# Mixed mLSTM attention and mixture-of-experts kernel: two raw weight tiles decoded later, another order of units 0 to 5, other places for w1's loads

## Chip, cores and metric

One core of one Trainium2 chip runs the whole program. The metric is the device time of one execution in microseconds; the median of several runs is given. The kernel issues all of its instructions by hand-written orders on five engines: PE (TensorE), DVE (VectorE), ACT (ScalarE), POOL (GpSimd) and SP (SyncE, which issues the loads).

## The reference

Three stages follow one another. The first is an mLSTM attention over 4 batches, 8 heads, 768 tokens and heads of 40, which the kernel computes in chunks of 128 tokens:

```python
for t in range(S):
    m_new = np.maximum(f_gate[:, :, t] + m, i_gate[:, :, t])
    f_stab = np.exp(f_gate[:, :, t] + m - m_new)
    i_stab = np.exp(i_gate[:, :, t] - m_new)
    C = f_stab * C + i_stab * np.einsum('bhd,bhe->bhde', vt, kt)
    n = f_stab * n + i_stab * kt
    h_tilde = np.einsum('bhde,bhe->bhd', C, qt)
    denom = np.maximum(np.abs(nq), 1.0)
    y[:, :, t] = sigmoid(o_gate[:, :, t]) * h_tilde / denom
```

The second is a soft mixture of experts over the 3072 tokens of width 320: logits against phi, a softmax over the tokens for each of 32 slots, 8 experts with w1 (320 x 1024) and w2 (1024 x 320) on the slots, and a softmax over the slots to mix back:

```python
slot_input = softmax(x @ phi, over tokens).T @ x
h = np.maximum(slot_input[e] @ w1[e], 0.0)
slot_out[e] = h @ w2[e]
x = softmax(x @ phi, over slots) @ slot_out
```

The third is a feed-forward block of width 1024 on every token:

```python
h = x @ w_in
solu = h * softmax(h)
ln = (solu - mu) / np.sqrt(var + 1e-06) * g_ln
return ln @ w_out
```

w_in and w_out come as 64-bit floats; the kernel takes their bits and builds 32-bit floats on the chip.

## The kernel before

**Attention.** There are 24 units, unit i being chunk i // 4 of batch i % 4. Each has one load of q and k (`load_qk`, three DMAs into 3 buffers) and one of k, v and the output gate (`load_kvo`, 484 KB into 4 buffers). A unit's work is a list of short names, in an order written out by hand: `FIRST` for units 0 to 5, `ORDER[i % 4]` for the others; `ops(i)` maps each name to a function. Every engine issues its own instructions in that order, so a name that stands earlier in the list goes earlier into its engine's queue. In unit i, `R` (`pe_decay`, lines 229 to 234) makes the decays of unit i + 2 with PE: for each half of the heads a product of `gl` and `gr` (L233) and one that adds the causal mask (L234). `exp` takes their exponential on ACT, `scA` and `scB` make the scores of unit i + 1 on PE (L265), `wA` and `wB` multiply the two on DVE into `lb` (L269), `o0` to `o3` are unit i's products with the values (L283) and with the state C (L286), `u0` to `u3` the update of the state (L293). `num`, `den`, `sg` and `x` form the output of unit i - 1; `numa` is a copy of PE's result on ACT (L308) in chunk 0 and sums on DVE from chunk 1 on, `C` is the new state (ACT L339 in chunk 0, DVE L341 behind that).

**Gates.** The gates of all 768 tokens of a chunk row are worked on together on 128 partitions: `gate(lo, hi, k)` (lines 166 to 191) is step k of eight, a scan for the maxima (L170), subtractions, cumulative sums (L181), and at last step 7, which adds the last sum of each chunk, and step 8, which builds the decays of whole chunks (`dec`, L191). Tokens 0 to 127 are done ahead of unit 0, 128 to 255 in unit 0 (names `GA`), and 256 to 767 in units 0 to 5 (names `GB`), 512 columns at once; for these step 7 runs on POOL (L189) and step 8 on DVE, over four chunks. `gate_hi` and `gate_lo` split a value in a high and a low part, `gate_right` (L211, POOL, for chunks 1 and 2; ACT for later ones) and `gate_left` (L216, ACT) spread them into `gr` and `gl`, `pe_gate` and `gate_nat` turn them for the chunk's use. The tiles `gt`, `m`, `gp` and `dec` of the gates lie in the pool `p1`, which is closed after the attention.

**Decoding.** Ten raw tiles of 512 KB (`load_raw`, lines 455 on), five of w_in and five of w_out, are loaded in the odd units 1 to 19 into two buffers in turn (`raw_t` and the last tile of `w1s`, which w1 needs last). Raw n is decoded in units 2n + 2 and 2n + 3 by `decode` (lines 462 to 480): `D0` are two DVE instructions (L469, L470), `D1` and `D1b` two on ACT (L472, L474), `D2` and `D3` two on DVE (L476, L478), and `D4` one product on POOL (L480).

**Loads.** All loads are issued by SP in one queue, each once its place is free. Each unit's loads of the unit after next go first, then one w1 tile of 512 KB at the end of the units in `W1_UNITS` (18 of them; the first of the 19 tiles of `w1s` is loaded ahead of unit 0's work, and a twentieth, `w1l`, goes in unit 22 into the place of `raw_t`). w2 of expert 0 is loaded after unit 21, the seven others (1280 KB each) when the attention is over, in the order 2, 4, 6, 1, 3, 5, 7, into the pool `tl`, which takes the place of the closed pools `p1` and w1s. A tile's load waits until every user of each tile that lay there is done.

**Tail.** The products with w1 (L787), then those with w2 (L831; the even experts first, eight and then 56 products, and 64 for the odd ones), then the mixing back. Between them `wo` loses its mean (L834), is copied into `wh` on ACT (L839), and the rest goes to `wl` on DVE (L840); behind that DVE copies the result of w2, `so` (L848). At last a loop over 24 tiles of 128 tokens does the feed-forward block (from L898 on); there the elementwise tiles `e` have three buffers in the pool `fin`.

## Time and profile before

| | us |
|---|---|
| median of 3 runs (lowest, highest) | 299.53 (298.48, 299.69) |
| the profiled execution | 295.74 |
| its span | 293.6 |
| busy in the span: PE, DVE, ACT, POOL | 274.5, 236.8, 214.5, 151.8 |

The profile is one execution, recorded by the hardware; the span runs from its first instruction to its last. Its granted TensorE clock is 1.00 all the way, the full of its two levels (2.4 GHz). "Busy" counts an engine's instructions, and PE's are modelled at their ends. A page of the profile gives totals, costliest groups of instructions and a chain: the work that ended last, followed back through what released it. Other views take a stretch of time or a line of the code. The loads' share is the mean busy share of the core's 16 DMA engines. The attention runs from about 10 to 144 us, the tail to 178 us, and the last loop to the end.

### The profile page before, as it was taken

The numbers are of one execution on the slowest core, as the hardware profiler recorded it, in microseconds if no ns is written. First come the engines' busy times: TensorE is split into PE (matmuls) and PEld (weight loads), VectorE is DVE, ScalarE is ACT, GpSimd is POOL, SyncE is SP. The second block draws the span as 40 slices with busy tenths as digits, with TensorE's granted clock in tenths as the row PEclk, the third lists the DMA queues.
The fourth block names the chain that finished last, engine by engine and source line by source line (L and its number), as shares of the span: only waits on it lengthen the run. The fifth ranks groups of instructions, "written<-read, shape, count | busy, mean of one in ns | idle before, by whom it ended". The sixth has DMA issues, their size and how long they took to land.

```text
span 293.6 us, 8341 instructions
## 1 busy us (share of the span) xinstructions
PE 274.5 (93%) x3245; PEld 219.5 (75%) x3245; DVE 236.8 (81%) x499; ACT 214.5 (73%) x482; POOL 151.8 (52%) x180
## 2 busy tenths in 40 slices
...
GB/s 160 251 298 265 285 284 198 211 341 291 291 257 292 284 307 246 278 298 362 369 364 361 169 2 0 0 119 111 104 90 99 104 89 100 103 88 99 106 82 47
DMA packets 48791, 57.28 MB, mean 195 GB/s; under 512 B 26800, under 2 KB 38704, under 8 KB 48752
## 3 DMA queue, kind: packets, MB, share of 16 engines
...
q14 instruction: 13, 0.11, 0.1%
HBM read 47.03 MB, written 3.93 MB: 174 GB/s over the span
## 4 chain that ended last, share of the span: by engine, by line
PE 74%; DMA 10%; DVE 9%; ACT 2%; POOL 2%; SPq 1%; issue 1%; POOLq 0%; ACTq 0%
PE o L982 10%; PE o L979 10%; PE o L980 9%; PE po L283 6%; PE sc L265 6%; DMA qk<-qkp 4%; PE uT L944 3%; PE pr L286 3%; PE h L898 3%; PE so_ph L831 3%; DMA gt<-gates 3%; DMA w1s<-w1p 3%; PE xTp L350 2%; PE R L233 2%; PE R L234 2%; PE dps L293 2%
## 5 line engine op out<-in xcount | busy, mean ns | idle before, releaser
L979 PE MATMUL o<-wh,uh 128*128 128x320 f32 x192 | 60.0, 318 | 0.0
L980 PE MATMUL o<-wl,uh 128*128 128x320 f32 x192 | 57.9, 307 | 0.0
L982 PE MATMUL o<-wh,ul 128*128 128x320 f32 x192 | 47.6, 308 | 0.0
L950 POOL COPY up<-u 128x1024 uint16<-128x1024 uint16 x22 | 23.3, 1060 | 45.1 <-issue 23.0
L283 PE MATMUL po<-kvo,lb 128*64 128x41 f32 x768 | 38.3, 229 | 5.1 <-ACT num L308 3.4
L283 PEld LDWEIGHTS po<-kvo,lb 128*64 128x64 f32 x768 | 30.6, 137 | 11.5 <-ACT num L308 3.8
L980 PEld LDWEIGHTS o<-wl,uh 128*128 128x128 f32 x192 | 36.1, 188 | 1.0
L979 PEld LDWEIGHTS o<-wh,uh 128*128 128x128 f32 x192 | 36.0, 188 | 0.9
L960 POOL COPY uf<-tp 128x1024 uint16<-128x1024 uint16 x22 | 35.3, 1605 | 2.5 <-DMA tp<-up 2.4
L917 DVE SCALAR_TENSOR_TENSOR u<-h,e 128x1024 f32<-128x1024 f32 (+1 forms) x25 | 29.4, 1181 | 9.0 <-ACT e L910 8.9
L265 PE MATMUL sc<-qk 64*128 64x128 f32 x384 | 31.5, 288 | 2.3 <-DMA qk<-qkp 1.2
L982 PEld LDWEIGHTS o<-wh,ul 128*128 128x128 f32 x192 | 33.0, 187 | 0.1
L269 DVE TENSOR_TENSOR lb<-sc,lb 128x512 f32<-128x512 f32 x48 | 31.3, 675 | 1.7 <-PE sc L265 1.7
L265 PEld LDWEIGHTS sc<-qk 64*128 64x128 f32 x384 | 25.3, 187 | 8.9 <-issue 4.3
L903 DVE TENSOR_REDUCE st<-h 128x1 f32<-128x1024 f32 x24 | 29.3, 1220 | 1.4 <-PE h L898 1.4
L246 ACT ACTIVATE kvo<-kvo 128x320 f32<-128x320 f32 x48 | 22.6, 471 | 8.6 <-DMA kvo<-kvo 6.0
L910 ACT ACTIVATE e<-h,st 128x1024 f32<-128x1024 f32 (+1 forms) x25 | 26.7, 1069 | 2.8 <-DVE st L903 2.6
L929 ACT ACTIVATE e<-u,st 128x1024 f32<-128x1024 f32 x24 | 27.4, 1141 | 0.0
L238 ACT ACTIVATE lb<-R 128x1024 f32<-128x1024 f32 x24 | 24.4, 1015 | 3.6 <-PE R L234 3.5
L986 ACT ACTIVATE ob<-o,st 128x320 f32<-128x320 f32 x24 | 12.7, 528 | 18.8 <-ACT e L910 13.6
L254 POOL TENSOR_TENSOR kvo<-kvo,nat 128x320 f32<-128x320 f32 x24 | 19.8, 825 | 10.6 <-PE sc L265 4.5
L233 PE MATMUL R<-gr,gl 128*128 128x512 f32 x48 | 22.8, 531 | 1.1 <-ACT lb L238 0.7
...
## 6 DMA issues: line engine op xcount, KB each, us to landing
...
```

What stands on the lines that cost most here:

```text
L233: PE.matmul(U[u]["R"][:, a], gl_t[c % 2][:, b, :], gr_t[c % 2][:, a * NR:(a + 1) * NR, :], start=True, stop=False)
L265: PE.matmul(U[u]["sc", a][:, r, :], t[p, 0, r, :], t[p, 1, r, :], start=True, stop=True)
L269: V.tensor_tensor(out=lb[:, a * NR:(a + 1) * NR, :], in0=U[u]["sc", a], in1=lb[:, a * NR:(a + 1) * NR, :], op=ALU.mult)
L283: PE.matmul(U[u]["po"][t, 2 * r + a, :], U[u]["lb"][:, a * NR + r, t], va(u, 2 * r + a), start=True, stop=True)
L903: V.tensor_reduce(out=F[i]["st"][:, 0:1], in_=F[i]["h"], axis=AX.XY, op=ALU.max, negate=True)
L910: A.activation(out=F[i]["e"][:, c], in_=F[i]["h"].rearrange("p n f -> p (n f)")[:, c], func=AF.Exp, bias=st[:, 0:1], accum_out=st[:, acc:a ...
L917: V.scalar_tensor_tensor(out=F[i]["u"][:, c], in0=F[i]["h"].rearrange("p n f -> p (n f)")[:, c], scalar=1.0, in1=F[i]["e"][:, c], op0=ALU. ...
L929: A.activation(out=F[i]["e"], in_=F[i]["u"], func=AF.Square, bias=st[:, 3:4], accum_out=st[:, 5:6])
L960: G.tensor_copy(out=uf.rearrange("p k t -> p (k t)").bitcast(U16).rearrange("p (n two) -> p n two", two=2), in_=F[i]["tp"].rearrange("p tw ...
L979: PE.matmul(o, uh, wh[:, k, :], start=k == 0, stop=False)
L980: PE.matmul(o, uh, wl[:, k, :], start=False, stop=False)
L982: PE.matmul(o, ul, wh[:, k, :], start=False, stop=k == FC - 1)
```

## The change

Nothing is computed differently. What changes is places and orders:

- The tiles of the gates (`gt`, `m`, `gp`, `dec`) move from the pool `p1` into a permanent tile `ga` of 2560 columns. After the gates are done its first 2048 columns take raw tiles 3 and 4, and in the last loop two of the three buffers of `e`. `p1` becomes shorter, and the places of `w1s` and of the w2 tiles against each other shift.
- In the attention only eight raw tiles are decoded (`RAWS`: 5, 6, 7, 8, 9, 0, 1, 2, in units 6 to 21; the two buffers change roles). Raws 3 and 4 are loaded at the ends of units 16 and 18 (`LATE`) and decoded by `late_decode`, which stands behind w2's products and ahead of `wh` and `wl`.
- `FIRST` is written anew: no decodes in units 2 to 5; the copies of num and C of chunk 0's units stand at the end of their own unit; steps of the gates stand later, step 5 in two parts; all of `left` for chunk 2 in unit 5.
- The load of the gates of tokens 256 to 767 stands behind that of q and k of unit 3, no longer ahead of it.
- `gate_right` for chunks 1 and 2 is one DVE instruction of 64x1024 in place of two on POOL of 64x512. The lower half of `gr`'s second tile is copied on POOL and not on ACT.
- Steps 7 and 8 of the gates run for one chunk at a time, on DVE, when `ops(i)` is called for units 6, 8, 12 and 16.
- `pe_decay` issues both products with `gl` and then both with the causal mask.
- `W1_UNITS`: no w1 load ahead of unit 1, two at the ends of units 4 and 5, one in each of the units 6 to 15, then units 17 and 22; `w1l` in unit 20.

```diff
--- before
+++ after
...
  "D1b xT numa R C numb scA D3 D1 scB o0 den0 sig0 cd den1 u3 D2 den2 wA D4 o3 u0 sig1 sg exp wB xTc u1 u2 o1 o2 lraw x sig2 kw right",
 )
 FIRST = (
- "q4 o0 u0 o1 u1 L0 R o2 u2 o3 u3 exp L1 wA wB kw sig0 sig1 sig2 left GA7 GA8 GB1",
- "scA numa scB C den0 den2 sg x o0 u0 o1 u1 wA R o2 u2 wB exp o3 u3 sig0 right0 kw right1 GB2 GB3 lraw k4 sig1 sig2",
- "q5 xT numa scA C scB den0 xTc den2 sig0 R o0 sg x o1 gn gnc u3 wA o3 kw wB GB4 o2 exp u1 u2 u0 sig1 D0 GB5 sig2 ph",
- "k5 q6 D1b xT numa C scA D1 scB o0 den0 den2 sg x sig0 D2 D3 u3 wA GB6 R D4 o3 u0 sig1 exp wB xTc u1 GH0 u2 o1 o2 lraw sig2 kw",
- "k6 R sig0 numa GH1 GL0 scA C xT scB den0 den2 o0 u0 xTc exp wB o3 o2 GL1 sg wA right0 cd o1 sig1 x D0 right1 u1 u2 u3 kw sig2 lfa gl",
- "q7 k7 D1b xT C numa numb R scA D1 D3 den0 xTc den2 sig0 lfb D2 scB kw sg wA o0 wB x u1 cd o3 lt o2 sig1 u3 o1 u2 D4 exp lraw ltc u0 tm0 GB7 GB8 sig2",
+ "q4 o0 u0 o1 u1 L0 R o2 u2 o3 u3 exp n0 c0 L1 wA wB kw GA7 GA8 right0 sig0 sig1 sig2 left",
+ "scA scB den0 den2 sg x o0 u0 o1 u1 wA R o2 u2 wB exp o3 u3 n1 c1 kw k4 GB1 sig0 sig1 sig2 ph GB2",
+ "q5 xT scA scB den0 xTc den2 o0 sg x o1 R gn gnc u3 wA o3 kw wB o2 exp u1 u2 u0 n2 c2 GB3 GB4 sig0 sig1 GB5a sig2",
+ "k5 q6 xT scA scB den0 xTc den2 o0 sg x o1 R u3 wA o3 kw wB o2 exp u1 u2 u0 n3 c3 GB5b GB6 sig0 GH0 sig1 sig2",
+ "k6 R sig0 GH1 scA xT scB den0 den2 o0 u0 xTc sg x exp wB o3 o2 wA cd o1 GL0 GL1 right0 sig1 u1 u2 u3 kw sig2 gl",
+ "q7 k7 xT C numa numb R scA den0 xTc den2 sig0 left scB kw sg wA o0 wB x u1 cd o3 lt o2 sig1 u3 o1 u2 exp lraw ltc u0 tm0 sig2",
 )
-W1_UNITS = (0, 2, 3, 4, 6, 7, 8, 9, 10, 12, 13, 14, 15, 16, 18, 19, 20, 21)
+W1_UNITS = (1, 2, 3, 4, 4, 5, 5, 6, 7, 8, 9, 10, 11, 12, 13, 14, 15, 17, 22)
+RAWS = (5, 6, 7, 8, 9, 0, 1, 2)
+RAW1 = 6
+LATE = {16: 3, 18: 4}
 HALVED = (0,)
 FIN_START = "h:0 m:0 w:2 e0:0 e1:0 h:1 m:1 u0:0 u1:0 w:2 T0:0 e:1 T1:0 u:1 x0:0 y0:0 x1:0 h:2 m:2 y1:0 v:0 v:1 e:2"
 FIN = "o:-1 u:2 d:2 t:2 h:3 m:3 q:0 k0:0 T0:1 T1:1 k1:0 x0:1 g:1 x1:1 y1:0 y0:1 k2:0 k3:0 s:0 a4:0 a5:0 e:3 a6:0 a7:0 v:1 b4:0 b5:0 b6:0 b7:0"
 DT = range(2, 24)
+HALF = (slice(0, 64), slice(64, 128))
 ENG = {"x": "G", "cd": "G", "kw": "G", "sg": "V", "D4": "G", "C": "V", "xTc": "A"}
 
 
...
     nat = cpool.tile([128, NU, NS], F32, tag="nat", name="nat")
     gl_t = [cpool.tile([128, NB, T], F32R, tag=f"gl{n}", name=f"gl{n}") for n in range(2)]
     gr_t = [cpool.tile([128, NH, T], F32R, tag=f"gr{n}", name=f"gr{n}") for n in range(2)]
+
+    ga = cpool.tile([128, 2560], F32, tag="ga", name="ga")
 
     w1_ctx = ExitStack()
     w1pool = w1_ctx.enter_context(tc.tile_pool(name="w1pool", bufs=1))
...
     cd_t = fixed("cd", [128, NR, 2 * DV])
     C_t = [fixed("Cl", [128, NR, 2 * DV])] + C_t
     dsc_t = fixed("dsc", [128, 512], 1, I32)
-    gt_t = fixed("gt", [128, 2, S])
-    m_t = fixed("m", [128, S + 1], 1, F32R)
-    dec_t = fixed("dec", [32, NC, 16])
-    gp_t = fixed("gp", [128, T], 1, F32R)
-    fixed("gap", [128, 112])
+    gt_t = ga[:, 0:2 * S].rearrange("p (k t) -> p k t", k=2)
+    m_t = ga[:, 2 * S:3 * S + 1].bitcast(F32R)
+    gp_t = ga[:, 2308:2308 + T].bitcast(F32R)
+    dec_t = ga[0:32, 2440:2440 + 16 * NC].rearrange("p (c j) -> p c j", c=NC)
+    fixed("gap", [128, 96])
     dps = ps_o.tile([128, NR, 2 * DV], F32, tag="dps", name="dps")
 
     def load_qk(u):
...
             last = gf[0:32].rearrange("p (c t) -> p c t", t=T)[:, :, T - 1:T]
             if k == 7:
                 g = gi[0:32].rearrange("p (c t) -> p c t", t=T)
-                (G if lo > T else V).tensor_tensor(out=g, in0=g, in1=last.to_broadcast([32, n, T]), op=ALU.add)
+                V.tensor_tensor(out=g, in0=g, in1=last.to_broadcast([32, n, T]), op=ALU.add)
             else:
                 V.tensor_tensor(out=dec_t[:, lo // T:hi // T], in0=m16.unsqueeze(1).to_broadcast([32, n, 16]), in1=last.to_broadcast([32, n, 16]), op=ALU.mult)
 
...
             for j in js:
                 A.activation(out=gr_t[c % 2][0:64, j, :], in_=x[0:64], func=AF.Copy, scale=hsel[0:64, j:j + 1])
             return
-        G.tensor_tensor(out=gr_t[c % 2][0:64, js], in0=x[0:64].unsqueeze(1).to_broadcast([64, NR, T]), in1=hsel[0:64, js].unsqueeze(2).to_broadcast([64, NR, T]), op=ALU.mult)
+        V.tensor_tensor(out=gr_t[c % 2][0:64], in0=x[0:64].unsqueeze(1).to_broadcast([64, NH, T]), in1=hsel[0:64].unsqueeze(2).to_broadcast([64, NH, T]), op=ALU.mult)
 
     def gate_left(c, js=range(NB)):
         p = slice(64, 128)
...
         U[u]["R"] = ps_sc.tile([128, 2, NR, T], F32, tag="R", name=f"R{u}")
         for a in range(2):
             PE.matmul(U[u]["R"][:, a], gl_t[c % 2][:, b, :], gr_t[c % 2][:, a * NR:(a + 1) * NR, :], start=True, stop=False)
+        for a in range(2):
             PE.matmul(U[u]["R"][:, a], eyeb, causal.to_broadcast([128, NR, T]), start=False, stop=True)
 
     def st_exp(u):
...
     def load_w1(n):
         SP.dma_start(out=w1s[:, n, :], in_=w1p[n])
 
-    raws = (w1s[:, 18, :].bitcast(I32).rearrange("p (n two) -> p n two", two=2), raw_t)
-
-    def load_raw(n):
-        raw = raws[n % 2]
+    raws = (raw_t, w1s[:, 18, :].bitcast(I32).rearrange("p (n two) -> p n two", two=2))
+
+    def load_raw(n, raw):
         SP.dma_start(out=raw, in_=w64[n].bitcast(I32).rearrange("p (n two) -> p n two", two=2))
         RAW[n] = raw
 
...
     def decode(n, k):
         lo, hi = RAW[n][:, :, 0].bitcast(U32), RAW[n][:, :, 1]
         f = win[:, n, :] if n < 5 else wo.rearrange("p f d -> p (f d)")[:, 512 * (n - 5):512 * (n - 4)]
-        if k == 0:
+        if (n, 0) not in RAW:
             RAW[n, 0] = dsc_t
         sc = RAW[n, 0]
         if k == 0:
...
     load_kvo(1)
     load_qk(2)
     load_kvo(2)
-    load_gates(2 * T, S)
     G.tensor_copy(out=gl_t[0][0:64], in_=bsel[0:64].unsqueeze(2).to_broadcast([64, NB, T]))
     A.copy(out=gr_t[0][64:128], in_=hsel[64:128].unsqueeze(2).to_broadcast([64, NH, T]))
     G.tensor_copy(out=eyeb, in_=ident)
...
     for a in range(2):
         pe_scores(0, a)
     load_qk(3)
+    load_gates(2 * T, S)
     load_kvo(3)
-    load_w1(0)
     pe_decay(0)
     st_exp(0)
     pe_gate(0)
...
     st_exp(1)
     for a in range(2):
         pe_scores(1, a)
-    A.copy(out=gr_t[1][64:128], in_=hsel[64:128].unsqueeze(2).to_broadcast([64, NH, T]))
     for a in range(2):
         st_w(0, a)
     st_sig(0)
...
         G.memset(x[:, DM + 1:384], 0.0)
         G.memset(x[:, DM:DM + 1], 1.0)
     G.tensor_copy(out=gl_t[1][0:64], in_=bsel[0:64].unsqueeze(2).to_broadcast([64, NB, T]))
+    G.tensor_copy(out=gr_t[1][64:128], in_=hsel[64:128].unsqueeze(2).to_broadcast([64, NH, T]))
     G.memset(sbd, 0.0)
 
     def load_phi():
...
         if nx2:
             T["R"] = lambda: pe_decay(i + 2)
             T["exp"] = lambda: st_exp(i + 2)
-        dn = (i - 2) // 2 if 1 <= i < 22 else -1
-        if dn >= 0:
+        dn = (i - RAW1) // 2
+        if 0 <= dn < len(RAWS):
             if i % 2 == 0:
-                T["D0"] = lambda: decode(dn, 0)
+                T["D0"] = lambda: decode(RAWS[dn], 0)
             else:
                 for n, k in (("D1", 1), ("D1b", 1.5), ("D2", 2), ("D3", 3), ("D4", 4)):
-                    T[n] = lambda k=k: decode(dn, k)
+                    T[n] = lambda k=k: decode(RAWS[dn], k)
         if i < 6:
             for k in range(1, 9):
                 T[f"GA{k}"] = lambda k=k: gate(TOK, 2 * TOK, k)
...
                 T[f"L{k}"] = lambda k=k: gate_lo(TOK, 2 * TOK, k)
                 T[f"GH{k}"] = lambda k=k: gate_hi(2 * TOK, S, k)
                 T[f"GL{k}"] = lambda k=k: gate_lo(2 * TOK, S, k)
-                T[f"right{k}"] = lambda k=k: gate_right(i // 4 + 1, slice(NR * k, NR * k + NR))
+            T["right0"] = lambda: gate_right(i // 4 + 1, None)
+            T["GB5a"], T["GB5b"] = lambda: gate(2 * TOK, 4 * TOK, 5), lambda: gate(4 * TOK, S, 5)
+            T[f"n{i}"], T[f"c{i}"] = lambda: st_num(i, (0,)), lambda: st_state(i)
         elif b and c + 2 < NC:
             js = range(4 * b - 8, 4 * b - 4) if c == 1 else range(3 * b - 3, min(3 * b, NH))
             T["right"] = lambda: gate_right(c + 2, js)
-        T["lfa"], T["lfb"] = lambda: gate_left(2, (0, 1)), lambda: gate_left(2, (2, 3))
-        nl = {0: 1}.get(i, c + 1 if b == 0 and i > 4 else NC)
+        nl = {0: 1, 5: 2}.get(i, c + 1 if b == 0 and i > 4 else NC)
         if nl < NC:
             T["left"] = lambda: gate_left(nl)
         ng = {2: 1, 6: 2}.get(i, c + 1 if b == 0 and i > 4 else NC)
         if ng < NC:
+            if ng > 1:
+                for k in range(7, 9):
+                    gate(ng * TOK, ng * TOK + TOK, k)
             T["gn"] = lambda: pe_gate(ng)
             T["gnc"] = lambda: gate_nat(ng)
-        if i % 2 == 1 and i < 20:
-            T["lraw"] = lambda: load_raw((i - 1) // 2)
+        if i % 2 == 1 and 0 <= i + 1 - RAW1 < 2 * len(RAWS):
+            T["lraw"] = lambda: load_raw(RAWS[(i + 1 - RAW1) // 2], raws[(i + 1 - RAW1) // 2 % 2])
         g = (i - 5) // 4
         if g >= 0:
             for k in range(3):
...
         if len(FIRST) <= i < NU - 2:
             load_qk(i + 2)
             load_kvo(i + 2)
-        if i == NU - 2:
+        if i == NU - 4:
             SP.dma_start(out=w1l, in_=w1p[19])
         T_ = ops(i)
         for t in (FIRST[i] if i < len(FIRST) else ORDER[i % NB]).split():
             if t in T_:
                 T_[t]()
-        if i in W1_UNITS:
-            load_w1(1 + W1_UNITS.index(i))
+        for n, u in enumerate(W1_UNITS):
+            if i == u:
+                load_w1(n)
+        if i in LATE:
+            n = LATE[i]
+            k = n - 3
+            load_raw(n, ga[:, 1024 * k:1024 * k + 1024].bitcast(I32).rearrange("p (n two) -> p n two", two=2))
         if i == NU - 3:
             load_w2(0)
         if i >= NU - 2:
...
         w2s[e] = tl.tile([128, FC, DM], F32, tag=f"w2s{e}", name=f"w2s{e}")
     for e in order:
         load_w2(e)
+    RAW[3, 0] = ga[:, 2048:2560].bitcast(I32)
+    RAW[4, 0] = fin.tile([128, FC, 128], F32R, tag="uh", name="dsc4", bufs=2).bitcast(I32).rearrange("p k t -> p (k t)")[:, 0:512]
+
+    def late_decode(steps):
+        for s in steps.split():
+            n, k = s.split(":")
+            decode(int(n), float(k))
+
     wh = fin.tile([128, FC, DM], F32R, tag="wh", name="wh")
     wl = fin.tile([128, FC, DM], F32R, tag="wl", name="wl")
+    e_t = [fin.tile([128, DF], F32, tag="e", name="e")] + [ga[:, DF * k:DF * k + DF] for k in range(2)]
     def w2_mm(e2, fs):
         for f in fs:
             for m in range(4):
...
     hidden_ev(1, hidden_T(1))
     w2_mm(0, range(1, FC))
     w2_mm(1, range(FC))
+    late_decode("3:0 3:1.5 3:1 4:0 4:1.5 4:1 3:2 3:3 4:2 4:3 3:4 4:4")
     A.copy(out=wh, in_=wo)
     V.tensor_tensor(out=wl, in0=wo, in1=wh.bitcast(F32), op=ALU.subtract)
     scratch = fin.tile([128, DF], F32R, tag="u", name="scratch", bufs=3)
...
     def f_exp(i, n=None):
         st = F[i]["st"]
         if not n:
-            F[i]["e"] = fin.tile([128, DF], F32, tag="e", name=f"e{i}", bufs=3)
+            F[i]["e"] = e_t[i % 3]
         c, acc = (slice(0, DF), 1) if n is None else (slice(512 * n, 512 * n + 512), (1, 8)[n])
         A.activation(out=F[i]["e"][:, c], in_=F[i]["h"].rearrange("p n f -> p (n f)")[:, c], func=AF.Exp, bias=st[:, 0:1], accum_out=st[:, acc:acc + 1])
 
```

## Rows read from the trace of the kernel before

**Rows 1.** Stretches: length, busy us of PE, PEld, DVE, ACT, POOL, clock, DMA share, GB/s.
```profile
10.00:56.00 46.00, 37.94 (x608) 27.85 (x608) 40.55 (x74) 35.39 (x78) 25.64 (x41) 1.00 0.85 255
56.00:136.00 80.00, 78.03 (x1404) 59.77 (x1402) 73.14 (x158) 62.74 (x147) 42.96 (x50) 1.00 0.91 290
141.00:162.00 21.00, 20.30 (x200) 9.49 (x202) 12.61 (x31) 7.82 (x23) 3.11 (x6) 1.00 1.07 363
```
**Rows 2.** The chain of waits: start us, us, what.
```profile
46.36 2.59 DVE dec L191
...
120.68 7.66 DMA w1s<-w1p
128.35 7.09 DMA qk<-qkp
```

**Rows 3.** Waits of DVE and of PE, 10 to 60 us: total, times, longest.
```profile
DVE m L170 <- DMA gt<-gates: 3.2, 1, 3.2
...
PE po L283 <- ACT num L308: 3.4, 2, 2.9
```

**Rows 4.** Stretches, the tiles dsc and win alone: DVE, ACT, POOL (second row: PE, PEld first).
```profile
26.00:45.00 19.00, 3.13 (x4) 1.43 (x2) 1.28 (x1) 1.00 0.93 278
...
26.00:46.00 20.00, 0.00 (x0) 0.00 (x0) 3.71 (x4) 1.45 (x2) 1.28 (x1) 1.00 0.92 278
```

**Rows 5.** Groups of POOL by line and shape: busy us, mean ns, idle time before.
```profile
L211 POOL TENSOR_TENSOR gr<-gp,cst 64x512 fp32r<-64x512 f32 x2 | 2.5, 1258 | 0.0
```

**Rows 6.** DVE's instructions in order of time: start us, us, line, operation.
```profile
7.75 0.27 DVE L189 TENSOR_TENSOR gt<-gt 32x128 f32<-32x128 f32 x1
7.95 0.29 DVE L191 TENSOR_TENSOR dec<-cst,gt 32x16 f32<-32x16 f32 x1
...
13.84 0.81 DVE L189 TENSOR_TENSOR gt<-gt 32x128 f32<-32x128 f32 x1
...
27.68 0.42 DVE L470 TENSOR_SCALAR win<-w1s 128x512 int32<-128x512 int32 x1
...
36.78 0.69 DVE L269 TENSOR_TENSOR lb<-sc,lb 128x512 f32<-128x512 f32 x1 [0.81 <-PE sc L265]
...
39.88 1.96 DVE L470 TENSOR_SCALAR win<-raw 128x512 int32<-128x512 int32 x1
```

**Rows 7.** Stretches as in the first group, for the DMA's share and rate.
```profile
10.00:20.00 10.00, 6.88 (x112) 5.12 (x112) 6.45 (x15) 8.63 (x19) 4.04 (x18) 1.00 0.97 266
...
30.00:40.00 10.00, 8.03 (x133) 5.88 (x133) 9.01 (x15) 8.26 (x18) 6.53 (x7) 1.00 1.00 303
...
60.00:70.00 10.00, 10.00 (x199) 8.08 (x200) 9.83 (x23) 8.95 (x22) 5.45 (x8) 1.00 0.92 317
...
20.00:136.00 116.00, 109.09 (x1903) 82.50 (x1899) 107.24 (x218) 89.50 (x205) 64.55 (x73) 1.00 0.88 278
```

**Rows 8.** Line 234's idle time before its instructions: us, times.
```profile
  issue: 8.2, 38
```

**Rows 9.** The tail in order of time, DVE, ACT, PE and SP's queue.
```profile
166.61 2.83 DVE L840 TENSOR_TENSOR wl<-wo,wh 128x2560 fp32r<-128x2560 f32 x1 [2.63 <-ACT wh L839]
171.97 0.49 DVE L848 COPY so_sb<-so_ph 128x320 f32<-128x320 f32 x1 [2.54 <-PE so_ph L831]
...
164.23 2.35 ACT L839 CAST wh<-wo 128x2560 fp32r<-128x2560 f32 x1
...
160.41 1.90 PE L787 MATMUL ph<-w1s,sbd 128*8 128x512 f32 x16
...
163.64 8.26 PE L831 MATMUL so_ph<-w2s,h 128*8 128x320 f32 x120
...
133.85 22.94 SPq L483 DMA_DIRECT2D w2s<-w  x7
```

**Rows 10.** The first gates: SP's issue, DVE's first use.
```profile
0.72 0.67 SPq L160 DMA_DIRECT2D gt<-gates  x1
...
3.45 0.48 DVE L170 TENSOR_TENSOR_SCAN m<-gt,m 128x128 f32<-128x128 f32 x1 [2.12 <-DMA gt<-gates]
```

5 lines of the change are left out of this document (2 added, 3 removed).

## The prediction

> **What bounds the kernel now.** I read busy time by stretches first, then the chain of waits, then the waits and durations of what the change touches. From 178 us to the end TensorE is the bound in a loop that the diff doesn't touch, so what can be won lies ahead of that, and there the stretches differ [rows 1]. From 10 to 56 us (units 0 to 6) PE is busy for 37.94 us of 46.00 and stands for 8.06, while DVE is busy for 40.55, 88%. From 56 to 136 us PE is busy for 78.03 us of 80.00: it is the bound there, but DVE (73.14) and the DMA (share 0.91) are close behind. From 141 to 162 us w2 streams in at 363 GB/s beside PE's work. The chain [rows 2] shows the costliest instruction of units 0 to 6, one product of the gates (2.59 us of DVE), and from 120.68 on two transfers of 7.66 and 7.09 us, which lead up to the scores of the last unit. By waits [rows 3], DVE stood 3.2 us for the gates' transfer, PE 3.4 us for ScalarE's copy of num, 2.9 of it at once.
>
> **Units 0 to 6, what is removed.** Two of the decodes leave these units. By their two tiles both cost 3.13 + 3.71 = 6.84 us of DVE, 1.43 + 1.45 of ScalarE, and 1.28 of POOL each [rows 4]. The product over four chunks, 2.59 us [rows 2], goes; it is made by chunk later. The gates' load moves behind qk 3 on SP's queue and the first instruction that needs it to the end of unit 1: the 3.2 us wait [rows 3] goes, and what is late next is qk and kvo, ahead of which the gates stood. num and C of chunk 0 are copied at the end of their own unit: PE's 2.9 us [rows 3] goes, the copies are only moved. The first w1 load (512 KB) leaves the queue ahead of qk 4 and is made up by the second loads of units 4 and 5.
>
> **Added there.** gate_right for chunks 1 and 2 was four POOL instructions of 64x512, of some 1.26 us [rows 5]; it becomes two of 64x1024 on DVE, and lb, the denominators and PE's products wait behind it. The trace has no such DVE instruction. The nearest is DVE's 128x512 multiply, 0.69 us [rows 6]; twice that is 1.4, which I take for each; bounds 0.7 and 2.6, the latter the dearest DVE instruction of these units [rows 2]. That one line's price on DVE varies is seen in the decode: 1.96 us for raw 1, 0.42 for raw 0 [rows 6]. The Trainium skill names a cause that would speak against this move (SBUF — State Buffer, "SBUF: two separate sides"): DVE and GpSimd share a port pair, which one of them takes for a whole instruction. By that rule each of the two would also stand for up to one POOL instruction, for the pair some 2 us on the path and a sum of −2.8 instead of the one below (296.7, inside the main case's own range); the trace can't show it for this shape, and the bounds above don't come from it. gr_t[1]'s lower half moves from ScalarE to POOL, which is busy for 25.64 us of 46 [rows 1] and loses two decode steps and four gate_right: hidden; without that cover it would be two instructions of 1.26 [rows 5].
>
> **What it comes to.** DVE is left with 40.55 − 6.84 − 2.59 + 2.8 = 33.9 us. In 38 us, PE's own busy time, that is 89%, as dense as now, so DVE no longer forbids that these units shrink by all of PE's 8.06. The transfers do. From 10 to 56 us they moved 255 GB/s × 46 us = 11.73 MB [rows 1], 2.66 MB of it up to 20 us at 266 GB/s and a share of 0.97 [rows 7]: no room there. Up to unit 7 the change issues as many 512 KB loads as now (eight), so 9.07 MB remain. At the 303 GB/s of 30 to 40 us, where the share was 1.00 [rows 7], they take 29.9 us, and unit 7 starts near 49.9 instead of 56: **−6.1**. Bounds: at 317 GB/s (60 to 70 us [rows 7]) −7.5, and −8.06 at most for PE; at 278, the mean of 20 to 136 us [rows 7], 32.6 us and −3.4. I take 303 since the share over all of 10 to 56 us is 0.85 now [rows 1]: that is the room into which the loads move.
>
> **The middle, 56 to 136 us.** A unit's R is now made by gate product, causal product, and the same again; it will be both gate products, then both causal ones. The weights of the causal product waited "for issue" for 8.2 us in 38 cases [rows 8]; they load beside a running matmul, so most of that is hidden. Bounds 0 and 8.2; I take 0.05 us for each of 17 units, −0.9. The last two gate steps of chunks 2 to 5 go to DVE ahead of units 6, 8, 12 and 16, at 0.27 to 0.81 and some 0.29 us [rows 6], 2.2 to 4.4 in all; the units' first DVE work is queued behind, PE waits for that, and where its slack doesn't cover it, it costs. I take +0.6 (0 to 2.2). Ahead of qk 23 there is one 512 KB load more than now (w1's last moves from unit 22 to 20). From 20 to 136 us 278 GB/s × 116 us = 32.2 MB moved [rows 7]; 32.8 MB in 110 us need 298, under the 303 and 317 seen. Since loads are issued only as buffers come free, some units will wait for qk: +0.7 (0 to 3).
>
> **The tail.** Two raw tiles are loaded at the ends of units 16 and 18, where the gates' last readers are done, and decoded behind the w2 products in program order. DVE is idle for 2.63 us ahead of wl and for 2.54 ahead of the copy of so at 171.97 [rows 9]; it is free from 164. Into that go 6.84 us of decode [rows 4], or 5.3 with both raws at the 0.42 of raw 0 [rows 6]; ScalarE does four steps of 0.72 before wh (2.35 us), and wl (2.83) needs wh [rows 9]. In order: DVE's first steps 164.0 to 166.8, ScalarE's last step to 167.6, wh to 170.0, DVE's second steps to 169.5, wl to 172.8: +0.9 for the copy of so (0.3 to 1.8). The raws' place also shifts the w2 tiles by 208 columns: the tile loaded last now covers the end of w1's, so its load waits for w1's last product, 160.41 + 1.90 = 162.3, where now all are issued by 133.85 + 22.94 = 156.8 [rows 9]. It is first used after 56 of the 120 products from 163.64, at 163.64 + 56 × 8.26 / 120 = 167.5 [rows 9]. The first 128 KB of the gates are issued at 0.72 and used at 3.45 [rows 10], 2.7 us, of which 0.4 is their bytes at 363 GB/s; with 2.3 + 3.6 us for 1280 KB the tile lands at 168.2, 0.7 late (−0.5 to 2). wl is late in the same time, so only the later of the two counts: **+0.9** for both. By the Trainium skill (DMA: Bandwidth & Descriptors, "Anatomy of one DMA — SWDGE (gpsimd) path") a transfer is some 2.0 us and its bytes at 436 GB/s, fitted on another path; this tile would then be an estimated 5.0 us under way, land at 167.3 and be in time, and the tail stays at wl's 0.9.
>
> **Sum.** −6.1 − 0.9 + 0.6 + 0.7 + 0.9 = −4.8 us on the profiled execution's 295.74 (span 293.6 and 2.1 around it): 290.9. The median of the runs shown, 299.53, stands 1.3% above that execution, as the sum then does: **294.7 us**.
>
> **Rivals.** *The loads keep their mean rate.* At 278 GB/s unit 7 starts 3.4 us earlier instead of 6.1: −2.1 in all, 297.4 us. For it: 266 GB/s at a share of 0.97 from 10 to 20 us; against it: 303 later [rows 7]. Chance 0.17.
> *Slower: the DMA sets the attention's end, as it does at unit 23 now.* Its chain is 14.75 us of transfers up to the last scores [rows 2]. If 32.8 MB come at 278 GB/s all the way, the early microseconds are given back in waits for qk, the load that is more costs 0.52 MB / 278 GB/s = 1.9 us, and the tail's 0.9 stays: +2.8, 302.4 us. It decides below 285 GB/s, where 32.8 MB take 115.1 us and the tail makes up the difference. Against it: a share of 0.91 in the middle [rows 1], so there is room in most units. Chance 0.11.
> *The late decode decides.* With DVE's eight instructions behind each other at 6.84, waits for ScalarE between, and the tile of w2 at its upper bound, the copy of so comes near 175: +3 instead of +0.9, −2.7 in all, 296.8 us. For it: 1.96 for raw 1 [rows 6]; against it: POOL has little else to do then. Chance 0.08.
> *It doesn't do what it says.* The early units wait for qk and kvo as long as they did for DVE, which now idles instead: 299.5. Against it: the share of 0.85. Chance 0.03.
>
> **How the numbers follow.** Main case 0.61, with a range of its own from 291 to 298. A measurement of this kernel can tell about 0.5%, 1.5 us, from no change. Faster by more: 0.60 + 0.11 + 0.05 = 0.76; within: 0.01 + 0.05 + 0.03 + 0.03 = 0.12; slower: 0.11 + 0.01 of the second case = 0.12. Low end: −7.5 in the early units and −2 for R, the other terms as they are, give −7.3; with the middle's two losses at nothing −8.6, 290.8: I set 290.5. High end: −3.4 in the early units, nothing for R and 3 for the denser loads give +1.1, 300.6, some way towards the slower case: 300.5.
>
> **What would show it.** Right: unit 7's first product near 50 us, no wait of DVE for the gates over 1 us, a DMA share over 0.9 from 20 to 50 us, less "issue" ahead of the causal weights, wl's end before 173. Wrong: waits of PE for qk of several us between 90 and 130 (the slower case), unit 7 at 53 (the first rival), so's copy after 174.

## The result and the profile after

The changed kernel takes 292.5 us (median of 4 runs, 291.27 to 293.66) against 299.0 (4 runs) for the kernel before: a ratio of 0.9854, 95% interval 0.9804 to 0.9904. Two later comparisons, beside other runs of the kernel before, gave 0.9841 (0.979 to 0.9893) and 0.9824 (0.976 to 0.9889). The forecast of 294.7 on 299.53 was a ratio of 0.984. A ratio compares only those executions of the two kernels that were in the faster of two states, so it isn't the quotient of the medians, which are over all executions.

The traced execution took 293.66 us, span 291.9. That is only 1.7 us under the span of the trace before: single executions of either kernel lie up to 2% apart, so the parts are read stretch by stretch here, and from several traces.

The stretches of the kernel after, the answers to [rows 1], columns as there:

```profile
10.00:51.00 41.00, 37.48 (x610) 27.23 (x609) 33.43 (x71) 31.92 (x73) 17.96 (x35) 1.00 0.94 285
51.00:132.00 81.00, 78.56 (x1403) 59.01 (x1403) 74.75 (x160) 63.32 (x146) 42.96 (x50) 1.00 0.90 290
137.00:158.00 21.00, 20.30 (x204) 9.40 (x206) 12.65 (x30) 7.62 (x22) 3.31 (x6) 1.00 1.01 340
```

The early units got shorter with the same work on PE: it stands still for 3.5 us (41.00 − 37.48) instead of 8.06. DVE's 33.43 us answer the 33.9 of the prediction; the DMA's share rose from 0.85 to 0.94. The middle is as it was. Unit 7's first product with the values, and the waits of DVE (10 to 60 us) and PE (8 to 140 us) there, answering [rows 3]:

```profile
51.10 0.43 PE L289 MATMUL po<-kvo,lb 128*64 128x41 f32 x7
...
DVE ga L176 <- DMA ga<-gates: 0.9, 1, 0.9
...
PE po L289 <- PE sc L272: 2.2, 3, 1.0
PE sc L272 <- DMA qk<-qkp: 1.4, 3, 0.8
```

Unit 7 starts at 51.10 instead of 56.07. The gates' wait is down from 3.2 to 0.9 us, the wait for ScalarE's num is gone, and waits for qk have come in. The chain of waits, 8 to 60 and 60 to 180 us (start, us, what), shows two transfers that now bind, qk 7 and the last w2 tile:

```profile
34.76 7.50 DMA qk<-qkp
...
158.22 7.49 DMA w2s<-w
165.75 4.47 PE so_ph L853 x58
```

And the tail, DVE, ACT, POOL, PE, and SP's queue in order of time, answering [rows 9]:

```profile
159.68 0.72 DVE L474 TENSOR_SCALAR ga<-ga 128x512 int32<-128x512 int32 x1
...
164.24 0.70 DVE L483 SCALAR_TENSOR_TENSOR dsc<-ga,dsc 128x512 int32<-128x512 int32 x1
165.81 2.94 DVE L863 TENSOR_TENSOR wl<-wo,wh 128x2560 fp32r<-128x2560 f32 x1 [0.87 <-ACT wh L862]
170.26 0.49 DVE L871 COPY so_sb<-so_ph 128x320 f32<-128x320 f32 x1 [1.51 <-PE so_ph L853]
...
163.47 2.31 ACT L862 CAST wh<-wo 128x2560 fp32r<-128x2560 f32 x1
...
156.21 1.90 PE L800 MATMUL ph<-w1s,sbd 128*8 128x512 f32 x16
...
159.44 4.49 PE L853 MATMUL so_ph<-w2s,h 128*8 128x320 f32 x62
165.75 4.47 PE L853 MATMUL so_ph<-w2s,h 128*8 128x320 f32 x58 [1.83 <-DMA w2s<-w]
...
163.81 2.26 POOL L485 TENSOR_TENSOR win<-win,ga 128x512 f32<-128x512 f32 x1 [1.93 <-DVE ga L483]
166.04 3.86 POOL L485 TENSOR_TENSOR win<-win,dsc 128x512 f32<-128x512 f32 x1
...
132.07 26.51 SPq L488 DMA_DIRECT2D w2s<-w  x7
```

The late decode fits into DVE's gap: its eight instructions end at 164.94 and wl at 168.75, 1.5 us before so's copy, which waits for PE. PE stops within the products with w2, because the last tile's load is issued only at 158.22, when w1's last product has ended (156.21 + 1.90 = 158.11). From the end of that product to the mixing it was 173.84 − 162.31 = 11.5 us before, and is 172.13 − 158.11 = 14.0 now. The 4.2 us with which the attention ended earlier become 1.7.

Where each traced execution stood, in us from the span's start, is in this table; "attention" is the same code in the six lower rows, since the two variants of the tail touch nothing ahead of it.

| kernel (trace) | unit 7 starts | unit 23 starts | w1's products start | w1's end to the mixing |
|---|---|---|---|---|
| before | 56.07 | 141.68 | 152.84 | 11.5 |
| before, again | 57.39 | 144.91 | 156.06 | 12.3 |
| after | 51.10 | 137.48 | 148.64 | 14.0 |
| after, again | 54.33 | 140.06 | 151.22 | 14.4 |
| after, third | 50.88 | 138.05 | 149.20 | 14.0 |
| split tile | 49.75 | 135.61 | 146.76 | 12.4 |
| split tile, so on ScalarE | 49.82 | 138.40 | 149.56 | 11.5 |
| the same, second | 49.71 | 137.57 | 148.72 | 11.5 |

The six executions with the changed attention start w1's products at 149.0 on average, the two of before at 154.5: 5.4 us for the attention, of which the tail takes some 2.2 back (14.1 on average in the three traces of the changed kernel, 11.9 in the two of before).

### The profile page after: what moved, and what is told of

Read it like the earlier page. It is cut to its first block, busy times and chain, and to the rows that moved or that the text cites. A ratio compares the mean times of both kernels' runs of the same rounds, so it can differ in the third digit from the quotient of the medians.

```text
span 291.9 us, 8339 instructions
## 1 busy us (share of the span) xinstructions
PE 275.8 (94%) x3245; PEld 218.3 (75%) x3245; DVE 237.6 (81%) x508; ACT 214.3 (73%) x481; POOL 150.2 (51%) x176
## 4 chain that ended last, share of the span: by engine, by line
PE 73%; DVE 10%; DMA 8%; POOL 3%; issue 2%; ACT 2%; SPq 0%; POOLq 0%; DVEq 0%; ACTq 0%
PE o L1002 10%; PE o L1003 10%; PE o L1005 10%; PE sc L272 6%; PE po L289 6%; DMA qk<-qkp 5%; PE uT L967 4%; PE h L921 3%; PE pr L292 3%; PE xTp L356 3%; PE R L239 3%; DMA w2s<-w 3%; PE R L241 2%; PE dps L299 2%; PE so_ph L853 2%
## 5 line engine op out<-in xcount | busy, mean ns | idle before, releaser
L940 DVE SCALAR_TENSOR_TENSOR u<-h,ga 128x1024 f32<-128x1024 f32 x16 | 19.6, 1223 | 5.5 <-ACT ga L933 5.5
L351 POOL TENSOR_TENSOR xx<-num,kvo 128x320 f32<-128x320 f32 x13 | 10.6, 812 | 20.2 <-DVE kvo L336 15.4
L292 PE MATMUL pr<-C,qk 128*64 128x82 f32 x240 | 20.9, 249 | 0.1
L994 DVE TENSOR_TENSOR ul<-uT,uh 128x512 fp32r<-128x512 f32 x26 | 17.8, 690 | 2.6 <-ACT uh L990 2.6
```

The source lines that it names most:

```text
L292: PE.matmul(U[u]["pr"][t, 2 * r:2 * r + 2, :].rearrange("p a d -> p (a d)"), qk_t[u % 3][:, 1, r, t], C_t[b][:, r, :], start=True, stop=True)
```

## The experiments

All change the kernel after, unless said otherwise. "From w1's first product to the mixing" in the expectations is a slip: the numbers there count from the end of w1's last product.

**Both kernels once more.**

> The changed kernel once more, unaltered, for a closer ratio and a second trace. If the result is what the profile showed, the ratio to the kernel before is 0.98 to 0.99 (about 294.5 against 299), unit 7 starts 5 us earlier than before, some 2 to 3 us of that are given back between units 7 and 17, and the products with w2 stand 1.5 to 2.5 us for the last w2 tile. If the first trace was an odd execution, the stand for the w2 tile or the slow units 6 to 10 are gone.

> The changed kernel a third time, beside the next one on the same chip: 0.98 to 0.988 of the kernel before; PE stands 1.8 to 2.2 us for the last w2 tile again, and from w1's first product to the mixing it is 14.0 to 14.4 us.

> The kernel before once more, for a second trace: the first one was an execution of 295.74 us where the median is near 298.5. If executions differ by how long the early units wait for transfers, as those of the changed kernel do (unit 7 at 49.8 to 54.3 us), unit 7 starts 1 to 4 us later than in the first trace (56.07), or units 7 to 23 take 1 to 4 us more than 85.6, and the tail is the same to 0.2 us. If the spread comes from the last loop, the tail or the loop differ.

Measured: 292.68 us and 0.9841 (0.979 to 0.9893); 294.71 us and 0.9824 (0.976 to 0.9889). PE stood for the w2 tile in all three traces of the changed kernel, 1.8, 2.2 and 1.8 us. Unit 7 was 5 us ahead in two of the three, and in the second only 1.7 (54.33). The second trace of the kernel before (299.72 us) has the same waits in its early units:

```profile
57.39 0.43 PE L283 MATMUL po<-kvo,lb 128*64 128x41 f32 x8
...
PE po L283 <- ACT num L308: 3.4, 2, 2.9
...
DVE m L170 <- DMA gt<-gates: 2.5, 1, 2.5
```

Its tail was expected to be the same to 0.2 us, and took 12.3 us against 11.5; why is not shown. What differs from execution to execution is above all the attention, by up to 4.6 us at unit 7 and 4.5 at its end; from the mixing to the end it is 119.7 to 120.0 us in each of them. In the one trace of the changed kernel with a late unit 7 (54.33) the clock fell. Stretches there, the clock ahead of the DMA's share:

```profile
37.00:40.00 3.00, 3.00 (x76) 2.38 (x75) 2.78 (x7) 0.86 (x3) 0.75 (x2) 1.00 0.81 261
40.00:43.00 3.00, 1.42 (x39) 1.18 (x35) 0.54 (x4) 2.96 (x9) 1.45 (x2) 1.00 0.93 318
43.00:46.00 3.00, 2.21 (x18) 1.80 (x18) 2.43 (x8) 0.78 (x2) 0.76 (x2) 0.78 1.02 355
46.00:49.00 3.00, 3.00 (x30) 1.70 (x30) 0.97 (x2) 0.80 (x3) 0.68 (x1) 0.65 1.01 257
```

PE was busy for 1.42 us of 3 at the full clock (2.4 GHz), and in the next six the granted clock was 0.78 and 0.65 on average, a mixture of that and of the lower level (1.2 GHz): 30 instructions in 3 us where 76 stood before. The chain puts unit 6's late start down to qk 7, which landed at 44.17; PE's idle time ahead of the fall was ended by ScalarE's copy of the logits (1.58 us) and then by qk (0.79). So a pause of PE can cost its wait and then some, whoever ends it. The second trace of the kernel before shows the same behind the wait of 2.9 us for num that the change removes: from 20.4 to 23.8 us its clock stood at the lower level.

**What holds the tail: the w2 tile alone, then with so's copy moved.** The tile of expert 7 is made of two, so that only the half over w1's end waits for w1:

```diff
+    w7lo = tl.tile([128, 4, DM], F32, tag="w7lo", name="w7lo")
+    w7hi = tl.tile([128, FC - 4, DM], F32, tag="w7hi", name="w7hi")
...
+    SP.dma_start(out=w7hi, in_=w2_7[:, 0:FC - 4])
+    SP.dma_start(out=w7lo, in_=w2_7[:, FC - 4:FC])
```

and in the second kernel also

```diff
-    V.tensor_copy(out=so, in_=so_ps[:, 0:DM])
+    A.copy(out=so, in_=so_ps[:, 0:DM])
```

> The last w2 tile (expert 7) is made of two tiles: rows of chunks 0 to 3 lie above w1's end and are loaded without waiting for w1's last product; chunks 4 to 7 lie over w1's end and are loaded behind it. Theory (the lateness of that one tile costs PE 2.5 us, and wl, ready 1.5 us before so's copy, costs at most 1): PE's stop between the w2 products is gone, so's copy is then held by wl on DVE, and the whole is 1.2 to 1.8 us faster than the changed kernel. Rival (the late decode is what holds the tail, the tile only fills the same time): less than 0.5 us. Third: the DMA is late in general and the stop moves to another tile: no gain.

> As the split of the w2 tile, and so's copy stands on ScalarE (idle from 166.7 to 171.3 in the changed kernel's trace), no longer behind wl on DVE. Theory: another 0.8 to 1.2 us, together 2.2 to 2.7 us faster than the changed kernel, about 0.978 of the kernel before. If wl does not hold so's copy, no more than the split alone.

> The split w2 tile and so's copy on ScalarE a second time, to see whether the 2.5 us of tail that its trace shows also come out in the times: from w1's first product to the mixing 11 to 11.5 us, and a ratio of 0.972 to 0.98 to the kernel before, 1 to 2.5 us under the changed kernel beside it. If times and trace go apart, less than 0.7 us.

Measured: 291.95 us, 0.9794 (0.974 to 0.9849); 291.97 us, 0.9805 (0.9759 to 0.9851); 291.12 us, 0.9813 (0.9737 to 0.989). With the split, PE makes the same products without a stop, in 9.77 us from first to last as in the first trace of the kernel before (12.3 in the kernel after), and wl is late next, as the prediction had it:

```profile
157.56 4.22 PE L864 MATMUL so_ph<-w2s,h 128*8 128x320 f32 x59
...
163.92 2.97 DVE L874 TENSOR_TENSOR wl<-wo,wh 128x2560 fp32r<-128x2560 f32 x1 [0.87 <-ACT wh L873]
166.82 0.48 DVE L882 COPY so_sb<-so_ph 128x320 f32<-128x320 f32 x1
```

PE's last product ends at 165.82 here and so is copied 1.0 us later, behind wl. On ScalarE (second trace of that kernel) it waits for PE alone:

```profile
167.85 0.43 ACT L882 COPY so_sb<-so_ph 128x320 f32<-128x320 f32 x1 [1.06 <-PE so_ph L864]
```

So the tile costs the tail 2.5 us and the late decode, by wl, at most 1.0 of the same time; both can be had back, 14.0 down to 11.5. The kernel of the next experiment adds a control: it keeps the tile and decodes nothing late, and its tail is 14.0 us too, with the same wait of PE (1.8).

The times don't show this gain clear of noise. Over the executions that the ratios use, the mean is 291.6 us for the last variant (12) and 292.4 for the changed kernel (14), 0.8 us apart with standard errors of 0.34 and 0.33, and the intervals of the ratios to the kernel before overlap. The 1.2 to 1.8 and 2.2 to 2.7 us that were expected did not come out: both kernels are 0.7 us under the changed kernel's 292.68 in the same series, and the ratios with so's copy moved, 0.9805 and 0.9813, stay above the expected ones. Nearest is the last expectation's "times and trace go apart". Both variants beat the kernel before clearly; whether they beat the changed kernel is open.

**The decodes back in units 2 to 5.** `RAWS` begins with 3 and 4 at unit 2, `LATE` is empty, `lraw`, `D0` to `D4` stand in `FIRST` where they stood before, and the late decode goes. Two more loads of 512 KB thus come into the early units, together with the decodes.

```diff
-RAWS = (5, 6, 7, 8, 9, 0, 1, 2)
-RAW1 = 6
-LATE = {16: 3, 18: 4}
+RAWS = (3, 4, 5, 6, 7, 8, 9, 0, 1, 2)
+RAW1 = 2
+LATE = {}
```

> The two raws are loaded in units 1 and 3 and decoded in units 2 to 5 as in the kernel before, with the rest of the change kept; nothing is decoded late. Theory (DVE's decode is what the early units can't carry): 6.84 us of DVE and two loads of 512 KB come back into some 38 us, unit 7 starts 2 to 4 us later than in the changed kernel, about 53.5 to 55; the tail still stops for the w2 tile, which doesn't depend on the decode. In all 1 to 3 us slower than the changed kernel. Rival (the transfers alone pace the early units, DVE has room): unit 7 within 1.5 us of the changed kernel's 51.1 and the whole within 1 us.

Measured: 296.6 us, 0.9963 (0.9925 to 1.0002): the change without this part is not clearly faster than the kernel before. Unit 7 starts at 54.02. The same 12 us in this kernel and then in the changed one:

```profile
28.00:40.00 12.00, 8.58 (x126) 5.87 (x121) 11.77 (x20) 8.10 (x16) 6.64 (x7) 1.00 0.99 317
...
28.00:40.00 12.00, 10.75 (x214) 8.13 (x212) 9.87 (x20) 10.15 (x23) 4.89 (x7) 1.00 1.02 308
```

DVE is busy for 11.77 of 12 us and PE for 8.58; without the decodes 9.87 and 10.75, at the same share of the DMA. From 10 to 56 us PE waits for no transfer in this kernel: its pauses go above all to "issue" (2.0 us) and to ScalarE (2.6). So the theory (DVE) holds, and the rival (only transfers pace these units) falls, although the edit adds transfers too. Unit 7 alone wouldn't show it, since one trace of the changed kernel has it at 54.33, and here too the clock fell, to 0.59 from 40 to 43 us. The times do: 3.9 us over the changed kernel's 292.68 in the same series, more than the 1 to 3 that were expected.

**The transfers in the early units.** No w1 load before unit 6, and then only the doubled loads moved:

```diff
-W1_UNITS = (1, 2, 3, 4, 4, 5, 5, 6, 7, 8, 9, 10, 11, 12, 13, 14, 15, 17, 22)
+W1_UNITS = (6, 7, 8, 9, 10, 10, 11, 11, 12, 12, 13, 13, 14, 14, 15, 15, 17, 20, 22)
```

```diff
+W1_UNITS = (1, 2, 3, 4, 5, 6, 7, 8, 9, 10, 11, 12, 13, 14, 15, 17, 19, 20, 22)
```

> No w1 load before unit 6, doubled loads in units 10 to 15 instead. It shows what units 0 to 6 take when the DMA has room. Theory (transfers pace them, DVE and PE would allow more): unit 7 starts at 48 to 49 (PE's busy time from 10 us), against 49.75 to 54.3 in executions of the changed kernel, and the loss moves to units 11 to 17, which become 0.3 us each longer or more. Rival (PE or DVE is the bound in units 0 to 6): unit 7 not before 49.5.

> The changed kernel with one w1 load at the end of each of the units 1 to 15 and of 17, 19, 20 and 22: none doubled in units 4 and 5. Theory (the loads in front of qk 7 make it late: it lands 4.4 to 7 us behind its issue and PE stands for it): one 512 KB load less in front is worth 1.5 to 1.7 us of landing, the first product of unit 6 comes by 43.5 or earlier (44.7 and 48.2 in two executions of the changed kernel) and qk 7 no longer ends late; of that some is given back by unit 23, since the later units carry the loads: 0 to 1.5 us faster in all. Rival (DVE or PE paces units 5 and 6): no difference before unit 8.

Measured for the first: 303.73 us, one run. Unit 7, a stretch of its early part and four of units 11 to 16, and PE's waits from 8 to 150 us:

```profile
49.35 0.37 PE L289 MATMUL po<-kvo,lb 128*64 128x41 f32 x6
...
30.00:50.00 20.00, 18.49 (x340) 14.07 (x341) 16.57 (x34) 15.42 (x38) 7.43 (x10) 1.00 0.57 162
...
71.00:78.00 7.00, 5.08 (x87) 3.68 (x85) 6.00 (x14) 3.54 (x9) 3.57 (x4) 1.00 1.02 314
78.00:87.00 9.00, 9.00 (x113) 7.20 (x113) 6.99 (x14) 7.02 (x18) 2.81 (x3) 0.62 0.97 291
...
100.00:108.00 8.00, 6.15 (x87) 4.53 (x87) 4.68 (x10) 4.11 (x10) 3.28 (x4) 0.86 0.99 321
108.00:117.00 9.00, 9.00 (x103) 7.00 (x101) 6.95 (x14) 6.85 (x14) 2.42 (x3) 0.55 0.70 210
...
PE sc L272 <- DMA qk<-qkp: 3.5, 4, 1.0
```

With the DMA only 0.57 busy, and no wait of PE for a load up to 50 us, unit 7 still starts at 49.35, 0.4 us ahead of the best traces of the changed loads: in this one trace that is the floor that the engines set. It is against the theory (48 to 49) and nearer to the rival (not before 49.5). The loads that were put off cost far more later: with two a unit the six units from 11 on take 45.7 us (32.7 in the changed kernel). PE's pauses from 74 to 77 us were ended by DVE (1.09 us by the last product of the chunk's gates, 0.82 by num), those from 98 to 106 us by qk (0.78, 1.02 and 0.83); behind both the clock fell, to 0.62 and 0.55. How much of the loss is the transfers' own is not separated.

Measured for the second: 295.11 us, 0.9902 (0.986 to 0.9943). Unit 7 starts at 49.77, as in the good traces of the changed kernel, and at 50.50 in the kernel of "All together" below, which has the same loads. So that the doubled loads in front of qk 7 make it late (51.10, 54.33) is not shown; unit 6's first product came at 43.66 and 44.39, not by 43.5, and at 43.59 to 48.22 with the doubled loads. The expected gain of 0 to 1.5 us did not come. Without the doubled loads time is lost at the end: PE waits from 115 to 140 us,

```profile
PE sc L272 <- DMA qk<-qkp: 2.4, 3, 1.0
```

where the changed kernel's trace has no wait for qk at all, and units 20 and 21 take 12.8 us (9.6). Units 17 to 22 together take 33.9 us in both traces without the doubled loads, 30.5 to 31.7 in the six of the table with them, and 32.8 and 32.5 in the kernel before. So the denser w1 loads in units 4 and 5 are worth having: they take loads from the late units, where the kernel before waited for qk [rows 2].

**All together.** The spread loads with the split tile and so's copy on ScalarE.

> The spread w1 loads, the split w2 tile and so's copy on ScalarE together. Theory: the tail from w1's first product to the mixing takes 11.5 us (14.0 to 14.4 in the changed kernel, 11.5 with the split and so's copy), and the early units gain up to 1.5 us: 1 to 3.5 us faster than the changed kernel, a ratio of 0.972 to 0.98 to the kernel before. If the load spread only moves waits, as with the split alone, 0.98.

Measured: 293.25 us, 0.9832 (0.9767 to 0.9898), no better than the changed kernel; the tail takes 11.5 us and the attention gives it away (unit 23 at 140.23). From 106 to 142 us PE waits for no qk here, and the chain runs over DVE's work, so the qk waits of the spread loads don't explain this trace; what does is open. The expectation of a gain from the spread was wrong.

**R's order, and gate_right.** The four products in the old order, and gate_right on POOL:

```diff
-        for a in range(2):
             PE.matmul(U[u]["R"][:, a], eyeb, causal.to_broadcast([128, NR, T]), start=False, stop=True)
```

```diff
-        V.tensor_tensor(out=gr_t[c % 2][0:64], ...)
+        G.tensor_tensor(out=gr_t[c % 2][0:64], ...)
```

> The changed kernel with R's four products in the order of before (gate, causal, gate, causal). By the prediction's step the new order is worth 0.05 us a unit, 0 to 0.17: the chain's pieces of R in one unit grow from about 0.92 to 0.97 us or more. By the first traces (0.24 + 0.23 + 0.23 + 0.23 = 0.93 before, 0.47 + 0.45 = 0.92 after) it is worth 0.01 us a unit, nothing that a time can show, and the rest of the trace agrees with the changed kernel's.

> The changed kernel with gate_right for chunks 1 and 2 on POOL, one instruction of 64x1024 each. In the changed kernel DVE takes 1.21 us for each, with no wait. By the prediction's sum it matters little here: POOL takes 2.2 to 2.6 us for each, unit 7 starts within 1 us of 49.8 to 51.1. By the rule of the shared port DVE's instructions beside it become longer, or it does, by up to a microsecond each.

Measured for R, from the chain of the old order, and of the changed kernel:

```profile
89.62 0.24 PE R L239
89.85 0.23 PE R L240
90.08 0.23 PE R L239
90.31 0.23 PE R L240
...
89.95 0.47 PE R L239 x2
90.42 0.45 PE R L241 x2
```

0.93 and 0.92 us a unit: 0.01 each, 0.2 in all. Units 7 to 22 take 86.8 us, 86.9 on average with the new order. The run took 294.58 us, which one run can't tell from the changed kernel. For gate_right, line 217 on POOL and on DVE (form, count: shortest, median, longest in ns):

```profile
L217 POOL TENSOR_TENSOR gr<-ga,cst x2: 1894/2115/2336, 16.6 to 34.1; 64x1024 fp32r<-64x1024 f32 x2
...
L217 DVE TENSOR_TENSOR gr<-ga,cst x2: 1207/1212/1217, 15.4 to 34.5; 64x1024 fp32r<-64x1024 f32 x2
```

1.21 us on DVE against 2.1 on POOL; unit 7 at 51.81, 293.49 us. One run can't tell this from the changed kernel either: which engine does it matters by no more than the spread.

Beside each other the two engines do get in each other's way, and the one that began second paid. Where DVE began first it was POOL: its instruction at 15.60 took 1.59 us beside DVE's from 15.38, where its line's mean is 0.82, and the two late POOL products took 2.26 and 3.86 beside DVE's work instead of 1.28. Where POOL began first it was DVE: with gate_right on POOL from 16.64 on, DVE's multiply by `rd` (L336) at 16.98 took 1.91 us, against 0.60 in the changed kernel, a little more than the microsecond of the expectation. In the changed kernel the same line takes 1.12 at 52.22, beside POOL's decode product from 51.71, and 0.49 where POOL stands still. The Trainium skill's shared port (SBUF — State Buffer, "SBUF: two separate sides") agrees with that: whichever of the two starts first has it for the whole instruction.

This changes how two rows of the kernel before are to be read. The 2.59 us of the product over four chunks at 46.36 [rows 2] and the 1.96 of raw 1's decode at 39.88 [rows 6] ran beside POOL instructions without a gap between them:

```profile
39.63 1.22 POOL L211 TENSOR_TENSOR gr<-m,cst 64x512 fp32r<-64x512 f32 x1
...
46.61 1.27 POOL L480 TENSOR_TENSOR win<-win,dsc 128x512 f32<-128x512 f32 x1
47.84 1.04 POOL L189 TENSOR_TENSOR gt<-gt 32x512 f32<-32x512 f32 x1
```

DVE's product ended at 48.95, just behind POOL's at 48.88, and the decode's line takes 0.41 where POOL stands still. So, by these rows, part of the DVE time that the change took out of the early units was waiting behind POOL, once behind gate_right itself (L211).

## Why the prediction was right, point by point

- **The total.** −4.8 us or 0.984 predicted, 0.9854, 0.9841 and 0.9824 measured, which is −4.4 to −5.3 us. The first and the last term decide it; with the two decodes back in the early units hardly anything is left of it (0.9963). The parts do not confirm it one by one: the traces' means give −5.4 up to w1's products and +2.2 for the tail, −3.2 together. With two traces of the kernel before, this is not enough to say where the rest lies, and in part the total is luck: a dearer tail than forecast is made up for somewhere that isn't shown.
- **Units 0 to 6, −6.1.** The attention's early gain is 5.0 us in the first trace, 5.8 between the means of six and of two, and unit 7 starts at 49.7 to 49.8 in three of six traces, where 49.9 was predicted. The reason was only half right. "The transfers do" is the sentence that failed: with the DMA at 0.57 the start is 49.35, so the engines' own order sets a floor of 6.7 us of gain, not PE's 8.06, and 303 GB/s gave nearly the same number by accident. The transfers have a part in how much of it is missed, 0.4 to 5 us by execution: the chain goes through qk 7 in the three traces of the changed kernel, and in the latest one the lower clock adds to it. That the decodes had to go for it is shown by the kernel that has them back: unit 7 at 54.02 and 3.9 us on the median. The 2.59 us of the four-chunk product and part of the decode were DVE standing behind POOL, so they are rightly taken off these units but are not what the work costs.
- **gate_right, 1.4 each taken:** 1.21. The port's price of 2 us on the path didn't come: DVE began first and POOL paid, off the path. The port spoke for the move at least as much as against it, since gate_right on POOL held DVE up, in the kernel before and in the experiment.
- **R's order, −0.9:** 0.01 us a unit. The waits "for issue" of [rows 8] went down a little (6.6 us in 24 cases, 8.2 in 38 before), but they lay under running matmuls: the chain's pieces are as long in either order. The lower bound was the value to take; the twentieth of a microsecond had no row behind it.
- **Chunk gates +0.6 and denser loads +0.7, with R +0.4 for the middle.** From unit 7 to unit 23: 85.6 and 87.5 us before, 85.7 to 88.6 (mean 86.9) after. 0.4 is inside that scatter, but it hides two parts. Units 7 to 16 took 52.9 and 55.0 us before and 54.7 to 57.3 (mean 55.7) after; units 17 to 22 took 32.8 and 32.5 before and 30.5 to 31.7 (mean 31.2) after. The denser loads, put at a loss, so gave time back at the end; what made units 7 to 16 longer, the chunk gates or the loads, isn't told apart. The chunk gates' steps on DVE come to 4.3 us in the first trace, near the upper end of the 2.2 to 4.4, since three of the four pairs ran beside POOL (1.3 us each, 0.4 alone).
- **The slower rival** (the attention ends when the DMA lets it) didn't come true, since the w1 loads are issued earlier: there is no wait for qk at unit 23, where PE stood 0.9 us for it before, behind the transfers of [rows 2]. Its mechanism is real, though: the two kernels that issue the loads later wait for qk there, and took some 10 us more (one run) and 2 us more than the changed kernel.
- **The tail, +0.9.** The order of the late decode was right, and each piece to 0.4 us once the 4.2 us are taken off by which w1's products end earlier, and wl's price is 1.0 (split tile) where 0.9 was said. What was mis-sized is the w2 tile: 0.7 late (−0.5 to 2) was said; PE waited 1.8 us for it and its products took 2.5 longer. The step took 2.3 us and 3.6 for the bytes, 5.9 from the issue; it was 165.75 − 158.22 = 7.5. Stretches of 1 us of the changed kernel show where it went, by their last two columns:

```profile
158.00:159.00 1.00, 0.94 (x14) 0.24 (x6) 1.00 (x1) 0.82 (x3) 0.14 (x1) 1.00 0.00 0
159.00:160.00 1.00, 1.00 (x16) 0.45 (x17) 0.72 (x3) 1.00 (x6) 0.61 (x1) 1.00 0.69 64
160.00:161.00 1.00, 1.00 (x20) 0.42 (x16) 1.00 (x2) 0.71 (x3) 1.00 (x3) 1.00 0.86 239
161.00:162.00 1.00, 1.00 (x20) 0.44 (x16) 1.00 (x2) 0.84 (x2) 0.88 (x1) 1.00 1.02 379
...
163.00:164.00 1.00, 0.92 (x14) 0.15 (x6) 1.00 (x3) 1.00 (x2) 0.18 (x1) 1.00 0.78 259
164.00:165.00 1.00, 0.00 (x0) 0.00 (x0) 0.94 (x2) 1.00 (x1) 1.00 (x1) 1.00 0.02 5
```

The queues had run empty. Nothing moves for a microsecond behind the issue, and the rate then climbs for two more; by the DMA's packets in the trace the first comes at 159.25 and the last bytes end at 164.15, and PE goes on 1.6 us behind. So the bytes took 4.9 us and the rest 2.6: it is the 3.6, the rate of a stream, that was most wrong. The other traces in which the queues were empty at the issue agree on that: in the second of the changed kernel and in the one with the decodes back it took 7.9 and 7.5 us in all, 6.0 and 5.8 of it for the bytes, with 0.8 and 0.7 behind them. Why a load alone moves more slowly than one in a stream is not shown.

By the Trainium skill (DMA: Bandwidth & Descriptors, "Anatomy of one DMA — SWDGE (gpsimd) path") some 2.0 us of a transfer are fixed, most of it behind the last byte. The sum is near what these traces show (1.7 to 2.6 us), but 1.0 of it lies ahead of the first byte. Its 5.0 us for this size, an estimate by its 436 GB/s, is too little: 7.5 were measured, since the bytes moved far below that rate.
